# Batch 0's loads ahead of everything else, TensorE transposes for all of batch 1, and probabilities times values as one matmul per head in two column groups

## The chip, the cores and the metric

The kernel runs on one core of a Trainium2 chip. The metric is the time of one execution on the device, in microseconds; lower is better. The profile is one further execution, taken by the hardware profiler. Its engines are TensorE (PE for matmuls, PEld for the weight loads that run beside them), VectorE (DVE), ScalarE (ACT), GpSimd (POOL) and the queue that issues DMAs (SP). The core has 16 DMA engines. PEclk is the share of its full clock that TensorE was granted.

## What is computed

Attention with a window of 32 in two kinds of mask, and then a feed-forward block whose input is first mixed along the sequence by a product of rank 32:

```
q, k, v: (8 batches, 8 heads, 576, 64); U (576,32), V (32,576); w_ch1 (512,2048), w_ch2 (2048,512)
scores = q k^T / 8                     # heads 0-3: 0 <= i-j < 32
                                       # heads 4-7: 0 <= i-j < 128 and (i-j) % 4 == 0
attn = exp(scores - max); attn /= sum(attn) + 1e-9
x = attn v, heads side by side         # (8, 576, 512)
u = x + (x^T U V)^T
out = u + relu(u w_ch1) w_ch2
```

## The kernel before

Tokens of the dilated heads are permuted so that their mask becomes a window of 32 as well. A **group** is four units of work; a unit is 64 queries of two heads at once. A batch has NGB = 9 groups, numbered g through all eight batches, so that batch 0 is g = 0 to 8 and batch 1 is g = 9 to 17.

Each group passes through these steps:

- `score` (L368): one matmul per unit. For batches 0 and 1 it is an f32 matmul of 128 rows (L392): q of the two heads stands in 128 weight columns, 96 keys stream past. Later batches use another layout and fp32r (L381), but for one group per batch.
- `soften` (L395): VectorE adds the mask and takes the maximum (L412), ScalarE takes the exponential and its sum (L416).
- `turn` (L424): the probabilities are transposed into `pt`. For g below PE_T = 12 TensorE does it, four transposes per group (L429) and one copy by VectorE (L433). From there on VectorE does it, eight block transposes per group (L445, or L442 where the group is wide).
- `weighted` (L448): the product with v. For each unit one f32 matmul (L453) with `pt` of both heads as 128 weight columns and v of both heads as 128 streamed columns. It computes a 128x128 result, of which the two 64x64 blocks on the diagonal, one per head, are used. An f32 matmul appears in the trace as two records with a weight load each. VectorE then multiplies by the reciprocal of the sum (L481) and writes into x, or for the dilated heads into `xp`, which DMAs scatter into x (L485).

After its nine groups a batch is mixed with U and V: `split` (L493), the matmuls of `t_mm` (L508, line 521, 64 weight columns each), `mix` (L539).

The feed-forward block runs over 12 chunks of 384 tokens. In each chunk, 16 slices of the hidden layer follow each other: `layer1` (L742, matmul L748) and `layer2` (L758, matmul L765), which make up most of TensorE's work. Between their matmuls `slot()` hands out the pieces of the attention of later batches: `queue` gives each piece a place in units of chunks. Batch 1 lies within chunk 0 (places 0 to HI1 - MARGIN = 0.55), batch 2 begins after it, and so on at a rate of a batch in 1.5 chunks.

**The beginning.** Before chunk 0, batch 0's attention and mixing run by themselves, with the preparation of the weights beside them. `weight_step` (L267) loads a piece of U, V or the 64-bit weights (L200, L202) and narrows it on ScalarE, VectorE and GpSimd. Loads are issued by SP in order. FETCH = 5 groups of q and k and four of v are issued ahead; `pre` (L591) issues the others while the groups run, into QKS = 4 buffers for q and k and VBS = 7 for v, in a pool `early` that is closed when batch 0 is done. From NE = 7 on q and k come in pairs of units instead, through `fetch` (L333), into TB = 3 buffers of the tag `qks`. The constant `wide_sb`, masks for batch 2 and later, has a place of its own from the start. Tile's scheduler orders the instructions of each engine at build time, so they need not stand in program order.

Of the kernel before, what the change touches and what calls it, by code (L numbers as in the profile page):

```python
# [10 lines left out]
F32 = mybir.dt.float32  # L11
F32R = mybir.dt.float32r
BF16 = mybir.dt.bfloat16
# [7 lines left out]
B, H, S, D = 8, 8, 576, 64  # L21
# [5 lines left out]
P = 128  # L27
QB = 64
NJ = S // QB
KB = QB + WIN  # L30
# [10 lines left out]
UNITS = 4  # L41
QK1 = P + KB
KW = P + WIN
# [4 lines left out]
NGB = len(TILES) // 2  # L48
# [11 lines left out]
H_ON_ACT = 3  # L60
XL_DVE = ((0, 1), (1, 1))
AHEAD = 2
FETCH = 5
POST_AT = 0.7
TAIL = 0.25
BLK = P // WIN
ZS = 2
NE = 7
QKB = 3
AHEAD_AT = 0.9  # L70
LO0 = 0.1
TB = 3
# [14 lines left out]
F_LAST = 13  # L87
RAWS = 4
VS = 4
QKS = 4  # L90
XPS = 4
VBS = 7
DVE_FROM = 2
TURN_AT = 0.5
TURN_GAP = 0.08
PT_ACT = ()
PE_T = 12
MASK_AT = (None, -16, 0, 16, 32, 48)
WIDE_AT = (None, 0, 16, 32, 48)
NEG = -8.0e9  # L100
# [50 lines left out]
def attention_moe_kernel(ctx: ExitStack, tc: tile.TileContext, qk1, qk2, vv, masks, wide, ident, ut, vt, w1, w2, out):  # L151
    nc = tc.nc

    const = ctx.enter_context(tc.tile_pool(name="const", bufs=1))
# [9 lines left out]
    def make_w(lo, hi, side):  # L164
        pool = tc.tile_pool(name=f"w{lo}", bufs=1, side=side)
        pool = ctx.enter_context(pool)
        n = hi - lo
        t1 = [pool.tile([P, KC, n * P], F32R, name=f"w1{i}_{lo}") for i in "hl"]
        t2 = [pool.tile([P, n, DM], F32R, name=f"w2{i}_{lo}") for i in "hl"]
        for f in range(lo, hi):  # L170
            fs = slice((f - lo) * P, (f - lo + 1) * P)
            held_w[f] = [t[:, :, fs] for t in t1] + [t[:, f - lo, :] for t in t2]

    HM = len(MASK_AT) // 2
    mask_sb = [work.tile([P, HM, KB], F32, tag="qk", name=f"mask{i}", bufs=QKB) for i in range(2)]
    spare = work.tile([P, QK2], F32, tag="qk", name="spare", bufs=QKB)
    wide_sb = const.tile([P, len(WIDE_AT), KW], BF16, name="wide_sb")
    id_sb = const.tile([P, P], F32, name="id_sb")
    us = const.tile([P, 9, 2 * RANK], F32R, name="us")
    vs = const.tile([P, P + S], F32R, name="vs")  # L180
# [117 lines left out]
    loaded = {}  # L298

    def load_qk(g):  # L300
        if g >= NE:
            if g == NE:
                for i in range(0, 2 * TB, 2):
                    fetch(UNITS * g + i)
        elif (g, 0) not in loaded:
            t = early.tile([P, UNITS, QK1], F32, tag="qk", name=f"qk{g}", bufs=QKS)
            nc.sync.dma_start(out=t, in_=qk1[g])
            loaded[g, 0] = t

    def load_v(g, i):  # L310
        if (g, 1, i) not in loaded:
            us_ = slice(2 * i, 2 * i + 2)
            if g < NGB:
                if i == 0:
                    t = early.tile([KB, UNITS, P], F32, tag="v", name=f"v{g}", bufs=VBS)
                    nc.sync.dma_start(out=t, in_=vv[g])
                    loaded[g, 1, 0] = t[:, 0:2]
                    loaded[g, 1, 1] = t[:, 2:4]
            else:
                t = work.tile([KB, 2, P], F32, tag="v", name=f"v{g}_{i}", bufs=3)  # L320
                nc.sync.dma_start(out=t, in_=vv[g][:, us_])
                loaded[g, 1, i] = t
# [10 lines left out]
    def fetch(n):  # L333
        if n >= UNITS * NG or n in raws:
            return
        if n < N2:
            if n % 2 == 0:
                raw = work.tile([P, 2, QK1], F32, tag="qks", name=f"qkr{n}", bufs=TB)
                nc.sync.dma_start(out=raw, in_=qk1[n // UNITS][:, n % UNITS:n % UNITS + 2])
                raws[n] = raw[:, 0]  # L340
                raws[n + 1] = raw[:, 1]
        else:
            raw = work.tile([P, QK2], F32, tag="qk", name=f"qkr{n}", bufs=QKB)
            m = QK1 if is_odd(n) else QK2
            nc.sync.dma_start(out=raw[:, 0:m], in_=qk2[n - N2][:, 0:m])
            raws[n] = raw
# [100 lines left out]

    def weighted(g, pt, ssum):  # L448
        b = g // NGB
        pv = psum.tile([P, UNITS, P], F32, tag="ps", name=f"pv{g}")  # L450
        for u in range(UNITS):
            v_sb = loaded[g, 1, u // 2]
            nc.tensor.matmul(pv[:, u, :], lhsT=pt[:, u, :], rhs=v_sb[:, u % 2, :], start=True, stop=True)  # L453
        nc.vector.tensor_scalar(out=ssum, in0=ssum, scalar1=1e-9, scalar2=None, op0=ALU.add)
        nc.vector.reciprocal(out=ssum, in_=ssum)
        moves = []
        xp = None
        for i in range(2):
            half, j = tile_of(g, 2 * i)
            us_ = slice(2 * i, 2 * i + 2)  # L460
            cs = slice(half * HALF_D, (half + 1) * HALF_D)
            if half == 0:
                t, row = divmod(b * S + j * QB, P)
                dst = x_tile(t)[row:row + QB, cs]
            else:
                if xp is None:
                    if b == 0:
                        xp = early.tile([P, HALF_D], F32, tag="xp", name=f"xp{g}", bufs=XPS)
                    elif b < SPLIT and g % 2:
                        xp = spare[:, 0:HALF_D]  # L470
                    else:
                        xp = work.tile([P, HALF_D], F32, tag="xp", name=f"xp{g}", bufs=1)
                    part = next(p for p, js in enumerate(DPART) if j in js)
                row = QB * DPART[part].index(j)
                dst = xp[row:row + QB]
                moves += [(t, to, n, row + r) for r, t, to, n in runs_of(b, half, j)]
            dst4 = dst.rearrange("p (u h d) -> p u h d", u=2, h=2)
            for h in range(2):
                rs = slice(QB * h, QB * (h + 1))
                norm = ssum[QB * i:QB * (i + 1), h::2] if is_wide(g) else ssum[rs, us_]  # L480
                nc.vector.tensor_tensor(  # L481
                    out=dst4[:, :, h, :], in0=pv[rs, us_, h * D:(h + 1) * D],
                    in1=norm.unsqueeze(2).broadcast_to([QB, 2, D]), op=ALU.mult)
        for t, to, n, r in sorted(moves):
            nc.sync.dma_start(out=x_tile(t)[to:to + DIL * (n - 1) + 1:DIL, HALF_D:], in_=xp[r:r + n])  # L485
        if moves and b == 0:
            split(b, part, 1, xp, slice(0, QB * len(DPART[part])))
# [96 lines left out]
    def batch_items(b):  # L584
# [3 lines left out]
        for s in range(NGB + LAG):  # L588
            g = NGB * b + s

            def pre(s=s, g=g):  # L591
                if b == 0:
                    for i in (g, g + 1, g + FETCH):
                        if i < NGB:
                            load_qk(i)
                    if g + FETCH - 1 < NGB:
                        load_v(g + FETCH - 1, 0)
                if 0 < s <= NGB:
                    load_v(g - 1, 0)
                if s >= LAG:  # L600
                    weighted(g - LAG, *held.pop(g - LAG))
                if b > 0 and 0 < s <= NGB:
                    load_v(g - 1, 1)

            def post(s=s, g=g):
                late = g - (NGB * b < PE_T)
                if late in state and late not in turned:
                    turned.add(late)
                    p_sb, _, ssum, _ = state.pop(late)
                    held[late] = (turn(late, p_sb), ssum)  # L610

            def some(us, g=g):
                for u in us:
                    score(g, u)
                for u in us:
                    n = UNITS * g + u
                    if n >= N2:
                        split_qk(n + LOOK)
                        fetch(n + LOOK + DMA_LOOK)
                    elif n >= UNITS * NE and n % 2 and n + 2 * TB - 1 < N2:  # L620
                        fetch(n + 2 * TB - 1)
                for u in us:
                    soften(g, u)

            step = UNITS if b < SPLIT else STEP
            units = [lambda us=range(u, u + step), some=some: some(us) for u in range(0, UNITS if s < NGB else 0, step)]
            if b < SPLIT:
                attn.append([lambda pre=pre, units=units, post=post: (pre(), [x() for x in units], post())])
            else:
                attn.append([pre] + units + [post])  # L630
# [43 lines left out]
    early_open = ExitStack()  # L674
    early = early_open.enter_context(tc.tile_pool(name="early", bufs=1))
    held_u.append(early.tile([P, len(DPART), 2 * RANK], F32R, name="us_d"))
    for g in range(FETCH):
        load_qk(g)
        if g == 0:
            for i in range(2):  # L680
                nc.sync.dma_start(out=mask_sb[i], in_=masks[:, HM * i:HM * (i + 1)])
        if g == 1:
            nc.sync.dma_start(out=id_sb, in_=ident)
        if g < FETCH - 1:
            load_v(g, 0)
    pre = batch_items(0)
    w_prio = [tc.cur_priority + W_OFF]
    for i, (_, it) in enumerate(pre):
# [11 lines left out]
    for _ in range(PRE_N):  # L700
        weight_step(NSMALL, NPIECE)
    tc.cur_priority = now
    early_open.close()
    make_w(F_MID, F_LAST, None)

    def ahead(stage):
# [164 lines left out]
```

## Time and profile before

| | |
|---|---|
| time, median of 3 runs | 1032.8 us (1031.57 to 1034.27) |
| the profiled execution's own time | 1032.92 us |
| its span in the trace | 1031.1 us |
| mean granted TensorE clock | 0.974 |
| first matmul of chunk 0 | at 69.54 us |
| first matmul of chunk 1 | at 177.86 us |

The span is the time between the first and the last instruction that the profiler saw; the 1.8 us that the run's own time is longer lie around it. Busy time counts each instruction from its start to its end. Consecutive matmuls overlap, so their durations add up to more than the time they take: what one costs in a row of its kind is read from the distance between starts. Below, "a group costs" means that distance summed over its records.

### The profile page before, as it was taken

Reading aid. Unit: us, or ns where it says so; the run is one execution under the profiler, and the core shown is the slowest. Engines: PE = TensorE matmul, PEld = TensorE weight load, DVE = VectorE, ACT = ScalarE, POOL = GpSimd, SP = SyncE. Lnnn points to the kernel's source line nnn. Section 1 sums busy time; section 2 is a strip of 40 time slices with the busy share of each in tenths; the row PEclk is TensorE's granted clock in tenths of the full one; section 3 lists DMA queues with packets and bytes.
Section 4 is the critical chain, followed back from the end, with each engine's and each line's share of the span. In section 5 each row is a group of like instructions: output and inputs, shape, how many; then the busy total and the mean of one; then the engine's idle time right before and its main releaser. Section 6 shows DMA issues by size and latency. Waiting matters only on the chain.

```text
span 1031.1 us, 17355 instructions
## 1 busy us (share of the span) xinstructions
PE 992.3 (96%) x5304; PEld 894.4 (87%) x5304; DVE 643.8 (62%) x2197; ACT 436.8 (42%) x1274; POOL 323.4 (31%) x519
## 2 busy tenths in 40 slices
PE   6769998999999999999999999999999999999998
PEld 5658887998899899998899898999889898999996
DVE  5888987877457863877557864777647874311211
ACT  5888874454244432444233532544324442111110
POOL 1476644353132630434122621335213431000000
PEclk9658999999999999999999999999999999999999
DMA  9767544243232433333232432424223321400000
GB/s 281 215 197 231 173 142 118 78 128 87 78 98 71 123 84 78 108 104 99 72 96 80 128 82 61 131 82 126 85 73 86 119 65 30 125 1 1 31 1 31
DMA packets 97197, 103.05 MB, mean 100 GB/s; under 512 B 12848, under 2 KB 84080, under 8 KB 97104
## 3 DMA queue, kind: packets, MB, share of 16 engines
q1 hardware_dynamic: 97104, 101.94, 34.6%
q8 instruction: 43, 0.70, 0.3%
q14 instruction: 50, 0.41, 0.1%
HBM read 79.86 MB, written 17.30 MB: 94 GB/s over the span
## 4 chain that ended last, share of the span: by engine, by line
PE 82%; DVE 10%; DMA 4%; ACT 3%; issue 1%; SPq 0%; POOL 0%; DVEq 0%; POOLq 0%; ACTq 0%
PE ph L748 36%; PE acc L765 35%; PE pv L453 5%; PE s L381 3%; PE t L521 2%; DVE pt L445 2%; DMA qk<-qk 1%; PE s L392 1%; DVE utl L582 1%; DMA qkr<-qk 1%; DMA v<-vv 1%; DVE v L217 1%; PE m L545 1%; ACT p L416 1%; DVE xp L481 1%
## 5 line engine op out<-in xcount | busy, mean ns | idle before, releaser
L765 PE MATMUL acc<-w2h,hh 128*128 128x512 f32 x576 | 229.4, 398 | 0.0
L765 PE MATMUL acc<-w2l,hh 128*128 128x512 f32 x576 | 228.5, 397 | 0.0
L357 POOL TENSOR_TENSOR qks<-qkr,qks 128x160 fp32r<-128x160 f32 x192 | 104.5, 544 | 376.8 <-ACT qks L356 254.4
L765 PE MATMUL acc<-w2h,hl 128*128 128x512 f32 x576 | 213.4, 397 | 1.6 <-DVE hl L754 1.6
L753 ACT ACTIVATE hh<-ph 128x384 fp32r<-128x384 f32 x192 | 93.6, 487 | 284.4 <-PE ph L748 274.6
L754 DVE SCALAR_TENSOR_TENSOR hl<-ph,hh 128x384 fp32r<-128x384 f32 x192 | 106.0, 552 | 167.5 <-ACT hh L753 167.0
L416 ACT ACTIVATE p<-p,nmax 128x160 f32<-128x160 f32 (+1 forms) x288 | 117.2, 408 | 137.4 <-DVE nmax L412 135.3
L748 PE MATMUL ph<-uth,w1h 128*128 128x384 f32 x768 | 175.3, 342 | 0.0
L748 PE MATMUL ph<-uth,w1l 128*128 128x384 f32 x768 | 174.6, 340 | 0.0
L748 PE MATMUL ph<-utl,w1h 128*128 128x384 f32 x768 | 173.3, 339 | 0.0
L748 PEld LDWEIGHTS ph<-uth,w1h 128*128 128x128 f32 x768 | 139.5, 190 | 15.0 <-ACT uth L581 0.3
L748 PEld LDWEIGHTS ph<-uth,w1l 128*128 128x128 f32 x768 | 136.8, 189 | 0.5
L748 PEld LDWEIGHTS ph<-utl,w1h 128*128 128x128 f32 x768 | 135.8, 188 | 1.5
L765 PEld LDWEIGHTS acc<-w2h,hl 128*128 128x128 f32 x576 | 108.1, 189 | 24.4 <-DVE hl L754 2.5
L442 DVE STREAM_TRANSPOSE pt<-p 32x128 f32<-32x128 f32 x384 | 115.9, 302 | 19.7 <-ACT p L416 14.5
L765 PEld LDWEIGHTS acc<-w2h,hh 128*128 128x128 f32 x576 | 109.2, 190 | 15.6 <-ACT hh L753 0.2
L765 PEld LDWEIGHTS acc<-w2l,hh 128*128 128x128 f32 x576 | 109.1, 189 | 14.8
L356 ACT CAST qks<-qkr 128x288 fp32r<-128x288 f32 x192 | 81.7, 430 | 84.7 <-PE s L381 58.7
L360 POOL TENSOR_TENSOR qks<-qkr,qks 64x128 fp32r<-64x128 f32 x192 | 90.1, 470 | 15.1
L409 DVE TENSOR_TENSOR p<-s,wide_sb 128x160 f32<-128x160 f32 x192 | 60.6, 319 | 46.6 <-PE s L381 44.6
L453 PE MATMUL pv<-v,pt 96*128 96x128 f32 x576 | 80.1, 283 | 3.8 <-DVE pt L445 1.7
L453 PEld LDWEIGHTS pv<-v,pt 96*128 96x128 f32 x576 | 77.2, 199 | 7.1 <-DVE pt L433 2.0
(68 smaller groups left out, 1052.9 us busy)
## 6 DMA issues: line engine op xcount, KB each, us to landing
qkr<-qk SPq DMA_DIRECT2D x192, 144.0 KB, 2.2
raw<-w SPq DMA_DIRECT2D x26, 512.0 KB, 5.1
v<-vv SPq DMA_DIRECT2D x126, 96.0 KB, 2.1
out<-x SPq DMA_DIRECT2D x36, 256.0 KB, 2.3
zd<-z SPq DMA_DIRECT2D x120, 64.0 KB, 1.9
xt<-zd SPq DMA_DIRECT2D x30, 256.0 KB, 2.8
qkr<-qk SPq DMA_DIRECT2D x22, 224.0 KB, 3.4
qk<-qk SPq DMA_DIRECT2D x7, 448.0 KB, 7.7
```

The lines of the kernel that those rows point to most:

```text
L356: nc.scalar.copy(out=t[:, 0:QK2], in_=raw)
L357: nc.gpsimd.tensor_tensor(out=t[:, QK2:], in0=raw[:, P:], in1=t[:, P:QK2].bitcast(F32), op=ALU.subtract)
L360: eng.tensor_tensor(out=t[lo, 0:P], in0=raw[lo, 0:P], in1=t[lo, 0:P].bitcast(F32), op=ALU.subtract)
L381: nc.tensor.matmul(sp, lhsT=t[:, 0:P], rhs=t[:, P:], start=True, stop=True)
L409: nc.vector.tensor_tensor(out=p_sb[:, u, :], in0=sp[:, 0:KW], in1=wide_sb[:, kind], op=ALU.add)
L416: nc.scalar.activation(out=p_sb[:, u, 0:w], in_=p_sb[:, u, 0:w], func=AF.Exp, bias=nmax[:, u:u + 1], scale=-1.0, accum_out=ssum[:, u:u + 1],)
L442: nc.vector.transpose(out=to[:, :, WIN * (r % 2):WIN * (r % 2 + 1)], in_=p_sb[rs, :, QB * s + WIN * k:QB * s + WIN * (k + 1)])
L453: nc.tensor.matmul(pv[:, u, :], lhsT=pt[:, u, :], rhs=v_sb[:, u % 2, :], start=True, stop=True)
L748: nc.tensor.matmul(ph, lhsT=w[:, k, :], rhs=u[:, k, :], start=(n == 0), stop=(n == len(seq) - 1))
L753: nc.scalar.activation(out=hh, in_=ph, func=AF.Relu)
L754: nc.vector.scalar_tensor_tensor(out=hl, in0=ph, scalar=0.0, in1=hh.bitcast(F32), op0=ALU.max, op1=ALU.subtract)
L765: nc.tensor.matmul(acc[i], lhsT=h[:, ss], rhs=w, start=(f == 0 and n == 0), stop=(f == FC - 1 and n == 2))
```

## The change

- Batch 0's nine groups of q, k and v are all issued first, in the order of the groups. q and k have nine buffers (QKS = 9, NE = 9), and v takes tiles of the pool `x` (16 buffers of 128 x 512 f32, of which the other users are the x tiles). The first half of the masks and the identity follow group 0's q and k, the second half follows group 2's. `pre` issues none of batch 0's loads any more. FETCH and VBS are gone. U, V, the weights and batch 1's first three pairs of q and k follow.
- PE_T is 18 instead of 12: groups 12 to 17, the last six of batch 1, are transposed by TensorE too, with VectorE's copy of line 433.
- `weighted` issues two matmuls for each unit, one per head: 64 weight columns of `pt`, 64 streamed columns of v. Head 0's result goes to partitions 0 to 63 and head 1's to partitions 64 to 127 of a tile of 4 x 64 columns, half as wide as before.
- `wide_sb` lives in a pool `rest` that is opened when `early` has been closed.

```diff
-FETCH = 5
-NE = 7
+NE = 9
-QKS = 4
+QKS = 9
-VBS = 7
-PE_T = 12
+PE_T = 18
...
     def load_qk(g):
-        if g >= NE:
-            if g == NE:
-                for i in range(0, 2 * TB, 2):
-                    fetch(UNITS * g + i)
-        elif (g, 0) not in loaded:
+        if (g, 0) not in loaded:
             t = early.tile([P, UNITS, QK1], F32, tag="qk", name=f"qk{g}", bufs=QKS)
...
-                    t = early.tile([KB, UNITS, P], F32, tag="v", name=f"v{g}", bufs=VBS)
+                    t = xpool.tile([P, UNITS, P], F32, tag="x", name=f"v{g}")[0:KB]
                     nc.sync.dma_start(out=t, in_=vv[g])
...
     def weighted(g, pt, ssum):
         b = g // NGB
-        pv = psum.tile([P, UNITS, P], F32, tag="ps", name=f"pv{g}")
+        pv = psum.tile([P, UNITS, D], F32, tag="ps", name=f"pv{g}")
         for u in range(UNITS):
             v_sb = loaded[g, 1, u // 2]
-            nc.tensor.matmul(pv[:, u, :], lhsT=pt[:, u, :], rhs=v_sb[:, u % 2, :], start=True, stop=True)
+            for h in range(2):
+                hs = slice(h * D, (h + 1) * D)
+                nc.tensor.matmul(pv[QB * h:QB * (h + 1), u, :], lhsT=pt[:, u, QB * h:QB * (h + 1)],
+                                 rhs=v_sb[:, u % 2, hs], start=True, stop=True)
...
-                    out=dst4[:, :, h, :], in0=pv[rs, us_, h * D:(h + 1) * D],
+                    out=dst4[:, :, h, :], in0=pv[rs, us_, :],
...
             def pre(s=s, g=g):
-                if b == 0:
-                    for i in (g, g + 1, g + FETCH):
-                        if i < NGB:
-                            load_qk(i)
-                    if g + FETCH - 1 < NGB:
-                        load_v(g + FETCH - 1, 0)
                 if 0 < s <= NGB:
                     load_v(g - 1, 0)
...
-    for g in range(FETCH):
+    for g in range(NGB):
         load_qk(g)
         if g == 0:
-            for i in range(2):
-                nc.sync.dma_start(out=mask_sb[i], in_=masks[:, HM * i:HM * (i + 1)])
-        if g == 1:
+            nc.sync.dma_start(out=mask_sb[0], in_=masks[:, 0:HM])
             nc.sync.dma_start(out=id_sb, in_=ident)
-        if g < FETCH - 1:
-            load_v(g, 0)
+        if g == 2:
+            nc.sync.dma_start(out=mask_sb[1], in_=masks[:, HM:])
+        load_v(g, 0)
...
     tc.cur_priority = now
+    for i in range(0, 2 * TB, 2):
+        fetch(UNITS * NGB + i)
     early_open.close()
+    rest = ctx.enter_context(tc.tile_pool(name="rest", bufs=1))
+    wide_sb = rest.tile([P, len(WIDE_AT), KW], BF16, name="wide_sb")
```

More of the change, by code (lines that the diff above doesn't have):

```diff
@@ L176, in attention_moe_kernel @@
     spare = work.tile([P, QK2], F32, tag="qk", name="spare", bufs=QKB)
-    wide_sb = const.tile([P, len(WIDE_AT), KW], BF16, name="wide_sb")
     id_sb = const.tile([P, P], F32, name="id_sb")
```

## The prediction

> **What bounds the kernel now.** I read the page first (span, slices), then the windows of the three stages, then waits and timeline inside each.
>
> ```profile
> span 1031.1 us, 17355 instructions
> PE   6769998999999999999999999999999999999998
> DVE  5888987877457863877557864777647874311211
> PEclk9658999999999999999999999999999999999999
> ```
>
> From the fourth slice on TensorE is busy 80% of a slice or more, and from the fifth on at nearly its full clock. VectorE is as busy in the first six slices (26 us each), and later mostly at 40 to 80%. So the run has a beginning in which no engine is full and a long rest that belongs to TensorE. The windows are cut at the first matmul of chunk 0 and of chunk 1 (columns: length, busy us and instructions of PE, PEld, DVE, ACT, POOL, then the granted clock, DMA share, GB/s):
>
> ```profile
> 0.00:69.50 69.50, 45.94 (x222) 38.34 (x223) 52.98 (x177) 49.31 (x142) 29.12 (x30) 0.73 0.78 235
> 69.50:177.80 108.30, 99.81 (x541) 88.17 (x540) 87.69 (x267) 82.43 (x221) 63.80 (x59) 0.94 0.55 167
> 177.80:1031.10 853.30, 846.55 (x4543) 767.86 (x4542) 503.17 (x1754) 305.11 (x914) 230.44 (x432) 1.00 0.29 80
> ```
>
> The first stage is batch 0 and the first weights: no engine is bound, the clock is 0.73. The second is chunk 0 with batch 1 in it. The third, 853 us, is TensorE's: 847 us busy, VectorE at 59%. In that third stage the largest wait that the list of waits has for a matmul is this one, so what is taken off TensorE's queue there comes off the end:
>
> ```profile
> PE acc L765 <- DVE hl L754: 1.6, 3, 0.6
> ```
>
> **Probabilities times values (pv), the term that decides.** One group in the third stage, with its neighbours (columns: start, time, count at the end):
>
> ```profile
> 303.68 0.31 PE L381 MATMUL s<-qks 128*128 128x320 f32 x1
> 303.83 1.05 PE L453 MATMUL pv<-v,pt 96*128 96x128 f32 x8
> 304.64 0.60 PE L748 MATMUL ph<-uth,w1h 128*128 128x384 f32 x2
> L453 PE MATMUL pv<-v,pt 96*128 96x128 f32 x576 | 80.1, 283 | 3.8 <-DVE pt L445 1.7 <-DVE pt L433 1.4 <-issue 0.6
> ```
>
> Eight records last 1.05 us from first start to last end, one alone 0.28 us (the mean of the last row). So starts lie (1.05 - 0.28) / 7 = 0.110 us apart, and a group costs 8 x 0.110 = 0.88 us.
>
> After the change a group has 16 records of 64 streamed columns. What one of them streams for comes from another f32 matmul, with 96 columns:
>
> ```profile
> 324.99 0.36 PE L392 MATMUL s<-qkr 128*128 128x96 f32 x2
> L392 PE MATMUL s<-qkr 128*128 128x96 f32 x136 | 22.1, 287 | 2.3 <-DMA qkr<-qk 2.3
> ```
>
> 0.36 - 0.28 = 0.080 us between its starts (the mean of 0.287 holds batch 0's at a lower clock, so one is taken as long as a pv record), so 128 columns take 0.110 and 96 take 0.080: in proportion, 64 take 0.055. One after another, 16 x 0.055 = 0.88 us: the change then saves nothing, since two heads of 64 columns stream as long as one matmul of 128. All of the gain must come from the two heads' halves of the array working at the same time. If they do, the order hi, lo of head 0, hi, lo of head 1 lets each second record start beside the first of the other head: 9 slots instead of 16, 9 x 0.055 = 0.50 us. The weight loads set another floor: the L392 records each load 128 columns and still start 0.080 us apart, so a load of 64 takes at most about 0.040 us, and 16 in a row at most 0.64 us. I take 0.57, between the two, as nothing in the trace shows two halves loading at once: 0.31 us saved per group, with 0.38 and 0.24 as the ends of this case.
>
> Whether halves cost something when TensorE enters and leaves them can be read from the mixing matmuls, which use 64 weight columns already (128*64 is rows by columns of the array):
>
> ```profile
> 236.13 0.69 PE L748 MATMUL ph<-uth,w1l 128*128 128x384 f32 x3
> 236.66 0.86 PE L521 MATMUL t<-xhl,us 128*64 128x256 f32 x6
> 237.36 0.34 PE L748 MATMUL ph<-uth,w1l 128*128 128x384 f32 x1
> ```
>
> Three ph take 236.66 - 236.13 = 0.53 us to the start of t, 0.177 each. The six t take 0.70 us to the start of the next ph, 0.117 each. Neither border shows anything extra, and weight loads of 64 columns stay hidden. What the trace doesn't show is an output on partitions 64 to 127 and the alternation between halves. Cost in the third stage, batches 2 to 7, 54 groups: 54 x 0.31 = 16.7 us less, all on TensorE's path, which had hardly a wait. The next engine in line there is VectorE, at 59%.
>
> **Batch 1's transposes.** Removed from VectorE are 6 groups x 8 block transposes, added are 6 copies there and 24 transposes on TensorE:
>
> ```profile
> L445 DVE STREAM_TRANSPOSE pt<-p 32x128 f32<-32x128 f32 x96 | 28.9, 301 | 3.9 <-ACT p L416 2.7
> L433 DVE COPY pt<-ptp 96x512 f32<-96x512 f32 x12 | 8.2, 682 | 3.0 <-PE ptp L429 2.7
> 15.96 0.27 PE L429 MATMUL ptp<-id_sb,p 128*96 128x128 f32 x1
> 17.56 0.38 PE L429 MATMUL ptp<-id_sb,p 128*96 128x128 f32 x2
> ```
>
> VectorE: 48 x 0.301 = 14.4 us away, 6 x 0.682 = 4.1 added, 10.3 us less of its 87.7 in chunk 0. TensorE: two in 0.38 us, less one alone (0.27), are 0.11 apart, so 24 x 0.11 = 2.6 us more. Behind each transpose on TensorE's queue stands the feed-forward; it waits if ScalarE's exponentials are late. But `turn` runs one group late, so they had a whole group's time. What VectorE's slowness costs TensorE now:
>
> ```profile
> 118.92 1.16 PE L453 MATMUL pv<-v,pt 96*128 96x128 f32 x8 [1.71 <-DVE pt L445]
> 120.79 0.78 PE L765 MATMUL acc<-w2h,hh 128*128 128x512 f32 x1
> 123.50 0.63 PE L765 MATMUL acc<-w2h,hh 128*128 128x512 f32 x1
> 241.03 0.40 PE L765 MATMUL acc<-w2l,hh 128*128 128x512 f32 x1
> 241.26 0.39 PE L765 MATMUL acc<-w2h,hl 128*128 128x512 f32 x1
> ```
>
> TensorE idles 1.71 us until 118.92. Soon after, seven acc matmuls stand between the starts 120.79 and 123.50, both counted, 2.71 / 6 = 0.45 us apart, where the third stage has 0.23 (the last two rows): half a clock, 6 x 0.22 = 1.3 us. I let both go with the wait: 3.0 us. With batch 1's own pv (9 x 0.31 = 2.8 us, by the sum above) and the 2.6 us added, chunk 0 becomes 3.2 us shorter. The ends of that: all 10.3 us of VectorE's time plus the 2.8, or, if the wait only moves to ScalarE, 0.2 us.
>
> The Trainium skill, TensorE: Matmul & The Clock Gate, Part 1, says that the clock is halved after an idle window of about 3.4 us. The idle time in the row is half as long, so by that rule the slow stretch had another cause and would stay: the time would then be 1.3 us longer.
>
> **Batch 0's loads.** Batch 0's later groups were fetched late:
>
> ```profile
> 2.60 0.42 SPq L307 DMA_DIRECT2D qk<-qk  x1
> 9.99 0.35 SPq L202 DMA_DIRECT2D raw<-ut  x1
> 18.22 0.33 SPq L307 DMA_DIRECT2D qk<-qk  x1
> 39.32 0.35 SPq L339 DMA_DIRECT2D qkr<-qk  x1
> 36.86 0.69 PE L392 MATMUL s<-qkr 128*128 128x96 f32 x4
> DVE p L412 <- PE s L392: 10.7, 5, 6.3
> qk<-qk SPq DMA_DIRECT2D x7, 448.0 KB, 7.7
> v<-vv SPq DMA_DIRECT2D x9, 192.0 KB, 7.7
> 19.06 0.62 ACT L209 ACTIVATE v<-raw 128x448 f32<-128x448 f32 x1 [0.75 <-DMA raw<-ut]
> 10.00:20.00 10.00, 9.90 (x67) 9.40 (x65) 7.01 (x44) 4.50 (x20) 0.00 (x0) 1.00 1.04 309
> ```
>
> The seventh group's q and k are issued at 18.22 us and the ninth group scores at 36.86. All nine now need 9 x (448 + 192) KB, about 5.9 MB: at the 309 GB/s of the last row, 19 us and, from the first issue on, some 21 us. Then VectorE is the next bound of batch 0. Its idle time in the first stage is 69.5 - 53.0 = 16.5 us; of that the first 6 pass before any score can exist, so about 10 can go at most. Of the 10.7 us in which it waits for scores, the first 6.3 is that same beginning, so some 4.4 us are the loads'. I take 4 us off the first matmul of chunk 0, ends 0 and 9. Each load moved forward is a load that U, V and the weights now stand behind: SP takes about 0.42 us apiece, 21 with masks and identity in some 9 us, so U's load is issued near 10 us as before (9.99), but lands behind 5.9 MB at some 22 us, where ScalarE now has it at 19.06: 3 us later. Covered by VectorE's and ScalarE's attention work of those microseconds; without that cover 3 us come back. Batch 1's first pairs and `wide_sb` go behind them too; they are first needed in chunk 0 and after it.
>
> The remaining edits are free: the pv tile half as wide is read in the same pieces (64 x 128 elements each), and v's tiles are given back to pool `x` before the weights' last pieces or batch 1's x need all 16.
>
> **The sum**, against the profiled execution's own 1032.9 us, which is 0.1 us from the median of the three runs: 1032.9 - 16.7 - 3.2 - 4 = 1009.0 us. With all ends good: 54 x 0.38 = 20.5, 13.1 and 9 less, 990; all bad but halves still parallel: 54 x 0.24 = 13, 0 and +3, 1023.
>
> **The rivals.**
>
> *The halves don't overlap.* Then a group stays at 0.88 us, or 0.96 if a record takes 0.060. For: no row of this trace shows two matmuls streaming at once. Against: nothing in the trace either; that the two heads use different weight columns and different partitions only makes it possible. Time: 0 to +5 us over 63 groups, chunk 0 without its 2.8 (0.4 left) and the loads as forecast: 1032.9 - 0.4 - 4 = 1028.5, to 1033.
>
> *Entering and leaving the halves drains TensorE.* There is one change of shape in the trace that does cost, to half of the rows:
>
> ```profile
> 241.78 0.30 PE L381 MATMUL s<-qks 128*128 128x320 f32 x1
> 242.02 0.33 PE L521 MATMUL t<-xhl,us 64*64 64x256 f32 x1
> 242.28 0.62 PE L748 MATMUL ph<-uth,w1h 128*128 128x384 f32 x2
> ```
>
> The s streams 0.15 us (303.68 to 303.83 above) and t starts 0.24 later, 0.09 more; t would take 0.117 and ph starts 0.26 later, 0.14 more. A round trip of 0.23 us, in 63 groups 14.5 us, turns 1009 into 1023. Against it: the 128*64 rows above show none of that. The Trainium skill, TensorEngine Tiling (Array Packing), Key Properties, says that changing the tiling mode, not just the tile, drains TensorE, and also that different tiles work in parallel. By the first the result would be this rival's; the 64*64 rows agree with it, the 128*64 rows don't.
>
> *Slower: the weight load of the other half can't be hidden.* If a load into the other half has to wait for the stream before it, each of the 16 records costs its stream and its load, with the nearest row 0.080 us: 16 x 0.080 = 1.28 us a group, 0.40 more than now. Over 63 groups 25 us: 1032.9 + 25 - 0.4 - 4 = 1053.5. It decides from the point at which the 4.4 us gained elsewhere are used up, 4.4 / 63 = 0.07 us a group, 0.060 us a record. For: 16 loads instead of 8, and f32's two records. Against: 64-column loads were hidden among the six t.
>
> **How the numbers follow.** About 0.3%, 3 us, is what a measurement of this kernel can tell from no change. Parallel halves without a drain: 0.60, since the loads and borders in the trace allow it and only parallelism itself isn't shown. No overlap: 0.20. Drain with overlap: 0.08. Slower: 0.12. Faster is the first and third case and most of the second's better half (0.08): 0.75. Within 0.3% the rest of the second: 0.12. Slower 0.13. The range runs from 1000, half the way from 1009 to all good ends (990), to 1031, which holds most of the no-overlap case (1028.5 to 1033); left out are the slower case and those outer ends.
>
> **What would show it.** pv: a group's 16 records within about 0.57 us and their neighbours undisturbed; chunks 1 to 9 shorter by about 6 x 0.31 = 1.9 us each. Transposes: no block transposes before chunk 1, VectorE some 10 us less there, no wait of pv for `pt`. Loads: the ninth group's score near 25 to 30 us instead of 36.86, first matmul of chunk 0 near 65.5. Wrong it is if pv's starts lie 0.055 us or more apart in sum, if gaps surround pv, or if chunk 0 begins no earlier because the weights or VectorE are late.

## The result and the profile after

| | before | after |
|---|---|---|
| median | 1033.26 us (6 runs, 1031.57 to 1034.27) | 1024.41 us (6 runs, 1021.52 to 1025.8) |
| ratio, 95% interval | | 0.9916 (0.9900 to 0.9933) |
| the profiled execution's own time | 1032.92 us | 1025.73 us |
| first matmul of chunk 0 | 69.54 us | 63.39 us |
| chunk 0, to the first matmul of chunk 1 | 108.3 us | 109.0 us |
| from there to the end of the span | 853.2 us | 851.6 us |

The change is faster by 8.9 us, 0.8%. The forecast was 24 us. The page of the changed kernel, in the lines shown of the one before:

```profile
span 1024.0 us, 18519 instructions
PE   6569998999999999999999999999999999999998
DVE  4977777887458854876557963777547874311211
PEclk9679998999999999999999999999999999999999
```

The picture is the same: TensorE holds the run from the fourth slice on, and nothing in these digits says what the halves did. The windows say where the time went, cut at the first matmuls of chunks 0 and 1 of this kernel:

```profile
0.00:63.39 63.39, 37.41 (x292) 28.32 (x292) 45.48 (x169) 39.27 (x125) 19.92 (x24) 0.78 0.74 218
63.39:172.39 109.00, 100.51 (x639) 86.13 (x639) 82.00 (x234) 91.10 (x238) 73.06 (x66) 0.94 0.61 192
172.39:1024.00 851.61, 844.38 (x4975) 747.29 (x4974) 504.39 (x1754) 303.33 (x913) 229.36 (x430) 1.00 0.28 80
```

Of the span's 7.1 us, 6.1 come from the beginning (forecast: 4), chunk 0 gives back 0.7 (forecast: 3.2 gained), and the third stage, where 16.7 were expected, yields 1.6. These 1.6 are less than the product itself gave there, for the third stage of the changed kernel begins at half the clock, and that of the kernel before did not. The first 4.2 us of the stage, the changed kernel's first:

```profile
172.39:176.60 4.21, 4.21 (x14) 4.21 (x14) 3.96 (x16) 1.70 (x7) 1.96 (x4) 0.50 0.46 127
177.86:182.10 4.24, 4.24 (x24) 4.24 (x25) 4.13 (x17) 1.87 (x7) 2.53 (x6) 1.00 0.62 168
```

Half of 4.2 us is 2.1; without that the stage would be some 3.7 us shorter.

One group of the product, with its neighbours in the queue:

```profile
206.34 0.34 PE L741 MATMUL ph<-uth,w1h 128*128 128x384 f32 x1
206.61 0.69 PE L448 MATMUL pv<-v,pt 96*64 96x64 f32 x16
207.22 0.61 PE L741 MATMUL ph<-uth,w1h 128*128 128x384 f32 x2
207.68 0.31 PE L374 MATMUL s<-qks 128*128 128x320 f32 x1
L448 PE MATMUL pv<-v,pt 96*64 96x64 f32 x1152 | 51.3, 232 | 2.9 <-DVE pt L426 2.7 <-DMA v<-vv 0.2
```

The 16 records last 0.69 us, one alone 0.23: their starts are 0.46 / 15 = 0.031 us apart on average, where one after another would need 0.055. (Single starts, which the row merges, come in twos 0.007 us apart; from one pair to the next it is 0.058 us, and 0.107 from the first to the second pair.) So the two halves do work at the same time. At that pace the 16 need 0.46 + 0.06 = 0.52 us. The loss is at the borders. A ph streams 0.175 us, but the product starts 206.61 - 206.34 = 0.27 us after it: 0.09 late. From its start to the next ph pass 0.61 us, 0.09 more than the 0.52, and the two ph that follow take 207.68 - 207.22 = 0.46 us instead of 0.35: 0.11 late. The visit costs 0.09 + 0.61 + 0.11 = 0.81 us, of which 0.29 are borders, against 0.88 before. (Counted in this way the group of the kernel before, at 303.83 us, costs the same 0.88 or 0.89: it starts 0.15 us after the s, which is not late, the ph follows after 0.81, and the two ph last 0.60 us, where two in a row last 0.177 + 0.34 = 0.52: 0.08 late.)

### The profile page after: what moved, and what is told of

The parts are those of the page before. It is cut to its first block, busy times and chain, and to the rows that moved or that the text cites. A ratio compares the mean times of both kernels' runs of the same rounds, so it can differ in the third digit from the quotient of the medians.

```text
span 1024.0 us, 18519 instructions
## 1 busy us (share of the span) xinstructions
PE 982.3 (96%) x5904; PEld 861.7 (84%) x5904; DVE 631.9 (62%) x2155; ACT 433.7 (42%) x1274; POOL 322.3 (31%) x519
## 4 chain that ended last, share of the span: by engine, by line
PE 85%; DVE 6%; DMA 5%; ACT 3%; issue 1%; SPq 0%; DVEq 0%
PE ph L741 38%; PE acc L758 36%; PE pv L448 3%; PE s L374 3%; PE t L517 2%; DMA qk<-qk 2%; DMA qkr<-qk 2%; PE m L541 1%; PE s L385 1%; DMA raw<-w 1%; DVE xhl L497 1%; DVE utl L578 1%; DVE pt L438 1%; ACT v L206 1%; ACT sign L208 1%
## 5 line engine op out<-in xcount | busy, mean ns | idle before, releaser
L758 PEld LDWEIGHTS acc<-w2h,hl 128*128 128x128 f32 x576 | 107.4, 189 | 24.8 <-DVE hl L747 2.8
L435 DVE STREAM_TRANSPOSE pt<-p 32x128 f32<-32x128 f32 x384 | 115.8, 302 | 16.5 <-ACT p L409 11.2
L758 PEld LDWEIGHTS acc<-w2l,hh 128*128 128x128 f32 x576 | 108.7, 189 | 15.7
L497 POOL TENSOR_TENSOR xhl<-x,xhl 128x256 fp32r<-128x256 f32 (+1 forms) x70 | 52.9, 778 | 78.0 <-ACT xhl L495 61.5
L215 POOL TENSOR_TENSOR v<-v,sign 128x512 int32<-128x512 int32 (+2 forms) x35 | 45.5, 1300 | 57.6 <-ACT sign L208 39.2
```

Of the source, the lines that this page charges most:

```text
L215: nc.gpsimd.tensor_tensor(out=vi, in0=vi, in1=s32, op=ALU.add)
L435: nc.vector.transpose(out=to[:, :, WIN * (r % 2):WIN * (r % 2 + 1)], in_=p_sb[rs, :, QB * s + WIN * k:QB * s + WIN * (k + 1)])
L497: eng.tensor_tensor(out=xl[rs], in0=x[rs], in1=xh[rs].bitcast(F32), op=ALU.subtract)
L758: nc.tensor.matmul(acc[i], lhsT=h[:, ss], rhs=w, start=(f == 0 and n == 0), stop=(f == FC - 1 and n == 2))
```

## The experiments

The theory after the comparison: the halves stream side by side, as forecast, and each visit to the half-wide shape costs TensorE about 0.3 us in drains, which eats the gain. The rivals: the halves save in full and another part of the change gives it back; or the lost time at the borders has nothing to do with the shape.

Each kernel is compared with the kernel before on the same chip (medians; ratio with its 95% interval):

| kernel | time | before beside it | ratio |
|---|---|---|---|
| pv_alone | 1027.9 | 1032.1 | 0.9952 (0.9933 to 0.9970) |
| no_pv | 1025.6 | 1032.1 | 0.9940 (0.9920 to 0.9960) |
| pe12 | 1025.8 | 1032.1 | 0.9939 (0.9920 to 0.9958) |
| pe18_alone | 1031.3 | 1032.1 | 0.9983 (0.9966 to 1.0001) |
| loads_alone | 1026.7 | 1032.9 | 0.9943 (0.9925 to 0.9962) |
| one_half | 1050.0 | 1032.4 | 1.0169 (1.0140 to 1.0197) |
| head_outer | 1040.8 | 1032.4 | 1.0080 (1.0055 to 1.0105) |
| wide_mid | 1048.4 | 1032.4 | 1.0149 (1.0116 to 1.0181) |
| wide_end | 1038.1 | 1032.4 | 1.0048 (1.0026 to 1.0070) |
| t_f32 | 1074.6 | 1032.9 | one run |
| u_early | 1022.4 | 1032.9 | 0.9901 (0.9881 to 0.9921) |
| paired68 | 1019.1 | 1032.9 | 0.9872 (0.9847 to 0.9897) |
| act_less | 1023.5 | 1032.9 | 0.9919 (0.9903 to 0.9935) |
| best | 1018.6 | 1032.9 | 0.9865 (0.9849 to 0.9882) |

**The parts by themselves.** First the product alone:

```diff
 (kernel before)
+            for h in range(2): ... one matmul per head, as in the change
```

> The kernel before with only the product split into two column groups; loads and transposes as before. Theory (the two halves do stream side by side, which saves some 0.36 us a group, but each entry into the half-wide shape and each way out of it drains TensorE, some 0.32 us a group): 63 groups x 0.04 us, so 2 to 3 us faster than before, about 1030 to 1031 us. Rival (the halves save their 0.3 us a group in full and the loads or the transposes of the change give it back): 17 us faster, about 1016.

Measured 1027.9, 4.2 us faster: a little more than the theory's 2 to 3, far from the rival's 17. Then the change without it:

```diff
 (changed kernel)
-            for h in range(2): ...
+            nc.tensor.matmul(pv[:, u, :], lhsT=pt[:, u, :], rhs=v_sb[:, u % 2, :], start=True, stop=True)
```

> The changed kernel with the product as one matmul of 128 columns per unit again; new loads and all of batch 1's transposes on TensorE stay. Theory (drains eat the saving of the halves): 2 to 3 us slower than the changed kernel, about 1027 us, the first matmul of chunk 0 still near 63 us. Rival (the halves save in full): 17 us slower, about 1041, slower than the kernel before.

Measured 1025.6; by the ratios, 0.9940 against 0.9916, 2.5 us slower than the changed kernel, and the intervals overlap. The rival's 1016 and 1041 are out: the product is worth some 2 to 5 us, not 17, and no other part of the change gives anything of that size back. The profiled executions agree: the third stage lasts 853.2 to 855.4 us in the four kernels with one matmul per unit (before, no_pv, pe18_alone, loads_alone) and 850.5 to 851.7 in the five with the product as in the change (changed, pv_alone, pe12, u_early, act_less).

```diff
 (changed kernel)
-PE_T = 18
+PE_T = 12
```

> The changed kernel with VectorE transposing groups 12 to 17 again. Theory (in chunk 0 ScalarE's narrowing of weights became the last to be done, so VectorE's 10 us are off the path and TensorE pays 2.6 us for the transposes): between 2 us faster and 1 us slower than the changed kernel, 1022 to 1025. Rival (the transposes give back what VectorE's wait cost, as forecast): 3 us slower or more, 1027 or above.

```diff
 (kernel before)
-PE_T = 12
+PE_T = 18
```

> The kernel before with only groups 12 to 17 transposed by TensorE. Theory of the forecast for this part by itself: 3.0 us of a wait and its half clock go, 2.6 us are added, so within 1 us of before, 1032 to 1034, VectorE some 10 us less busy in chunk 0. Rival (chunk 0 waits for VectorE more widely): up to 10 us faster, 1023. Other rival (the transposes wait for ScalarE on TensorE's queue): 2.6 us slower or more, 1036.

By the ratios the transposes are worth 2.4 us in the change (pe12, 0.9939 against 0.9916) and 1.8 us alone, and neither can be told from nothing; pe12 lies between its two expectations and tells no more. VectorE is relieved about as worked out: in chunk 0 of pe18_alone, from 66.57 to 173.16 us, it is busy 79.23 us, 8.5 fewer than the 87.69 of the kernel before.

```profile
66.57:173.16 106.59, 99.41 (x565) 89.15 (x565) 79.23 (x226) 82.07 (x223) 63.70 (x60) 0.95 0.56 171
```

The loads without the two other parts:

```diff
 (changed kernel)
-PE_T = 18
+PE_T = 12
-            for h in range(2): ...
+            nc.tensor.matmul(pv[:, u, :], lhsT=pt[:, u, :], rhs=v_sb[:, u % 2, :], start=True, stop=True)
```

> The kernel before with only the new order and buffers of the loads (and wide_sb's later place); product and transposes as before. Theory (the loads carry most of the change's gain): chunk 0 begins 6 us earlier, of which 1 us is lost in chunk 0, where ScalarE now has the weight pieces that it used to narrow before it: 5 us faster than before, 1027 to 1028. Rival (their gain is all lost in chunk 0, as the work is only moved): 1032 to 1033.

Measured 1026.7, 6.2 us faster: the loads carry most of the change. Alone, the three parts take off 0.48%, 0.17% and 0.57%, together 1.2%; the change with all three takes off 0.84%. Some of it may overlap, but the intervals are nearly as wide as the difference.

**The borders.** Is it the shape? One small matmul over all 128 columns goes into each group, once in the middle and once at the end (its result isn't used):

```diff
 (changed kernel)
-        pv = psum.tile([P, UNITS, D], F32, tag="ps", name=f"pv{g}")
+        pv = psum.tile([P, UNITS + 1, D], F32, tag="ps", name=f"pv{g}")
...
+            if u == 1:          # wide_mid; wide_end: u == 3
+                nc.tensor.matmul(pv[:, UNITS, 0:32], lhsT=id_sb, rhs=id_sb[:, 0:32], start=True, stop=True)
```

> The changed kernel with one small matmul over all 128 columns (32 columns streamed, its result unused) between units 1 and 2 of each group, so that each group leaves and enters the half-wide shape twice. Theory (each leaving and entering costs some 0.3 us): 0.3 us and 0.06 us for the matmul itself in 63 groups, some 23 us slower than the changed kernel, 1047. Rival (the gaps at the borders are not caused by the shape): as the next one, 1028.

> Control of the one before: the same small matmul after unit 3, where the shape changes anyway. Theory: only its own 0.06 us in 63 groups, 4 us slower than the changed kernel, 1028. Rival (the small matmul itself costs): as the one before.

A group of wide_mid, then one of wide_end:

```profile
199.80 0.31 PE L374 MATMUL s<-qks 128*128 128x320 f32 x1
200.04 0.45 PE L448 MATMUL pv<-v,pt 96*64 96x64 f32 x8
200.42 0.41 PE L451 MATMUL pv<-id_sb 128*128 128x32 f32 x2
200.76 0.45 PE L448 MATMUL pv<-v,pt 96*64 96x64 f32 x8
201.14 0.61 PE L743 MATMUL ph<-uth,w1l 128*128 128x384 f32 x2
```

```profile
195.35 0.31 PE L374 MATMUL s<-qks 128*128 128x320 f32 x1
195.59 0.69 PE L448 MATMUL pv<-v,pt 96*64 96x64 f32 x16
196.21 0.41 PE L451 MATMUL pv<-id_sb 128*128 128x32 f32 x2
196.45 0.60 PE L743 MATMUL ph<-uth,w1l 128*128 128x384 f32 x2
```

In wide_mid 1.10 us pass from the first product record to the ph, in wide_end 0.86. The same work, one visit more: 0.24 us. The small matmul itself costs more than I expected (0.86 instead of 0.61 us), so wide_end is 10 us slower than expected. The difference of the two times, 10.3 us over 63 groups or 0.16 each, is smaller than the 0.24 of the rows; the intervals of the two ratios allow both. The third stages of the two profiled executions, 875.2 and 861.1 us, are 14.1 apart, 0.26 in each of the 54 groups. One more visit does cost, so the gaps belong to the shape.

Is it the second half?

```diff
 (changed kernel)
-        pv = psum.tile([P, UNITS, D], F32, tag="ps", name=f"pv{g}")
+        pv = psum.tile([P, 2, UNITS, D], F32, tag="ps", name=f"pv{g}")
...
-                nc.tensor.matmul(pv[QB * h:QB * (h + 1), u, :], ...
+                nc.tensor.matmul(pv[0:QB, h, u, :], ...
...
-                    out=dst4[:, :, h, :], in0=pv[rs, us_, :],
+                    out=dst4[:, :, h, :], in0=pv[0:QB, h, us_, :],
```

> The changed kernel with both heads' results on partitions 0 to 63, so that all 16 records use the same half of the columns, as the mixing matmuls do. Theory (what drains TensorE is the use of the second half; work in the first half alone enters and leaves for nothing, as in the mixing matmuls): no pairs, 16 x 0.056 = 0.90 us a group and no gap at either border, 0.09 us more than the changed kernel's 0.81 over 63 groups: some 6 us slower than it, 1030. Rival (any f32 work with 64 weight columns drains): 0.90 + 0.32 us a group, 26 us slower, 1050.

```profile
196.17 0.31 PE L374 MATMUL s<-qks 128*128 128x320 f32 x1
196.41 1.15 PE L448 MATMUL pv<-v,pt 96*64 96x64 f32 x16
197.49 0.62 PE L741 MATMUL ph<-uth,w1l 128*128 128x384 f32 x2
197.94 0.36 PE L385 MATMUL s<-qkr 128*128 128x96 f32 x2
```

My theory of the second half fell: the time is the rival's, 1050.0. The s streams 0.15 us, the product starts 0.24 after it; the two ph take 0.45 instead of 0.35. The borders are those of the changed kernel although only the first half is used, as in the mixing matmuls that had shown none. And 16 records in one half take (1.15 - 0.23) / 15 = 0.061 us each from start to start, with the first one late, instead of 0.031: it is the other half that pairs them.

What then sets the mixing matmuls apart? They are fp32r, with 128 rows.

```diff
 (changed kernel)
-                t_ps[b, c], lhsT=u[rs], rhs=m[rs],
+                t_ps[b, c], lhsT=u[rs].bitcast(F32), rhs=m[rs].bitcast(F32),
```

> The changed kernel with the mixing matmuls of U in f32 instead of fp32r, same shapes: two records of 256 columns each instead of one. Only their borders matter. Theory (it is f32 that makes work with 64 weight columns drain TensorE, also in the first half and with 128 rows): the matmul before the first of a run is followed by its successor some 0.09 us late, and the matmul after the last one likewise, where fp32r showed nothing. Rival (the drain belongs to the 96 rows of the probabilities): no gap here. In time each of some 106 such matmuls outside batch 0 takes 0.43 us instead of 0.117, 33 us, and 20 us more with a drain at each of some 60 borders: 1058 without and up to 1078 with drains.

```profile
263.69 0.39 PE L758 MATMUL acc<-w2h,hh 128*128 128x512 f32 x1
263.92 0.40 PE L758 MATMUL acc<-w2l,hh 128*128 128x512 f32 x1
264.25 0.65 PE L517 MATMUL t<-xhl,us 128*64 128x256 f32 x2
264.82 0.44 PE L741 MATMUL ph<-utl,w1h 128*128 128x384 f32 x1
```

The acc before the t starts 0.23 us before its successor acc, but the t comes 0.33 us after that one: 0.10 late, in the same shape 128*64 that had no gap in fp32r. The two t records take 0.57 us to the ph, where 2 x 0.216 would do (256 columns at the f32 pace of the product, 0.055 us for 64, give 0.22): 0.14 late. The ph itself lasts 0.44 us, where one behind another ph lasts 0.34. So it is f32 in 64 weight columns, not the rows or the half; f32 alone doesn't do it, as the 128-column product of the kernel before enters without a gap. The time, 1074.6 us in a single execution, lies near the theory's upper number, 1078.

**Do pairs need neighbours?**

```diff
 (changed kernel)
-        for u in range(UNITS):
-            for h in range(2):
+        for h in range(2):
+            for u in range(UNITS):
```

> The changed kernel with the loops of the product exchanged: all units of head 0, then all of head 1, so that neighbours in the queue share a half. Theory (the pairs come from neighbours in different halves; matmuls start in order): starts 0.056 us apart except at the change of head, borders as in the changed kernel, 0.4 us more a group, some 25 us slower than the changed kernel, 1050. Rival (the halves work apart however they are queued): as the changed kernel, 1024.

```profile
199.25 0.31 PE L374 MATMUL s<-qks 128*128 128x320 f32 x1
199.49 0.97 PE L448 MATMUL pv<-v,pt 96*64 96x64 f32 x16
200.39 0.62 PE L741 MATMUL ph<-uth,w1l 128*128 128x384 f32 x2
```

From the first product record to the ph pass 0.90 us: more than the 0.61 of the changed kernel, less than one_half's 1.08. So 1040.8 lies between the two expectations. Single starts show why: twelve of the fifteen distances are 0.052 us or more and three are 0.004 to 0.006. The first of these three stands between the fifth and the sixth start. The sixth record lasts 0.270 us, as otherwise only the first of a half does (the first one in one_half, the first two in the changed kernel), where all others last 0.222: it is the first of head 1, and it starts ahead of the last three of head 0, which the kernel issues before it. So the halves need not be neighbours in the queue, and these matmuls do not start strictly in order, as the theory had it; but five of head 0's eight had started alone.

**Using it.** If a visit costs by itself, two groups in one visit should cost one drain:

```diff
 (changed kernel; from batch 2 on)
+            def both(s=s, g=g):        # at place i + 0.68 of every other step
...
+                gs = [i for i in (g - LAG, g - LAG + 1) if i < NGB * (b + 1)]
+                pvs = [product(i, held[i][0]) for i in gs]
+                for i, pv in zip(gs, pvs):
+                    weighted(i, *held.pop(i), pv=pv)
...
-                t = work.tile([KB, 2, P], F32, tag="v", name=f"v{g}_{i}", bufs=3)
+                t = work.tile([KB, 2, P], F32, tag="v", name=f"v{g}_{i}", bufs=6)
...
-                        xp = work.tile([P, HALF_D], F32, tag="xp", name=f"xp{g}", bufs=1)
+                        xp = work.tile([P, HALF_D], F32, tag="xp", name=f"xp{g}", bufs=2)
```

The maxima and sums of the softmax also get a third buffer from batch 1 on.

> The changed kernel with the products of two groups issued together from batch 2 on (five visits to the half-wide shape per batch instead of nine; v is loaded one step earlier into six buffers, xp has two). Theory (each visit costs 0.35 us beside 16 or 32 records in pairs 0.058 us apart): a double visit takes 1.28 us instead of 2 x 0.82, 24 of them save 8.6 us, and the later work of VectorE gives perhaps 2 back: 1016 to 1018. Rival (the gaps belong to each group, say to its wait for the transposes, not to the visit): as the changed kernel, 1024, or slower by VectorE's bunched work.

```profile
186.87 0.39 PE L776 MATMUL acc<-w2h,hl 128*128 128x512 f32 x1
187.10 0.39 PE L776 MATMUL acc<-w2h,hh 128*128 128x512 f32 x1
187.42 1.15 PE L447 MATMUL pv<-v,pt 96*64 96x64 f32 x32
188.50 0.50 PE L776 MATMUL acc<-w2l,hh 128*128 128x512 f32 x1
188.84 0.39 PE L776 MATMUL acc<-w2h,hl 128*128 128x512 f32 x1
```

A double visit costs 0.32 - 0.23 = 0.09, then 188.50 - 187.42 = 1.08, then 0.34 - 0.23 = 0.11: 1.28 us, instead of 2 x 0.81. The kernel takes 1019.1 us, 5.3 us less than the changed kernel (4.5 by the ratios), some 60% of the 24 x 0.34 = 8.2 us that the visits save. The theory of a price per visit holds; its 1016 to 1018 was a little low. Where the rest went is in the third stage and in the waits of its matmuls:

```profile
171.58:1017.40 845.82, 834.65 (x4975) 744.14 (x4974) 503.08 (x1754) 299.81 (x913) 227.93 (x430) 1.00 0.29 81
PE acc L776 <- DVE ssum L456: 2.6, 2, 1.4
PE ph L759 <- DVE utl L583: 2.2, 3, 0.8
```

The stage is 5.8 us shorter than the changed kernel's, although TensorE is idle for 845.8 - 834.7 = 11.2 us of it instead of 7.2, in waits for VectorE above all. No kernel has the added buffers without the pairing; but where TensorE was idle for 7.2 us and is now for 11.2, it isn't the buffers that took its time off.

**The beginning and chunk 0.**

```diff
 (changed kernel)
-PRE_AT = range(1, 7)
+PRE_AT = range(1, 6)
         load_v(g, 0)
+        if g == 4:
+            weight_step(0, NSMALL)
```

> The changed kernel with the loads of U and of the first half of V issued after the fifth group's q, k and v instead of after all nine. Theory (SP could not issue U's load until 19 us since the queue was full, and ScalarE stood idle half of the time from 20 to 30 us): ScalarE narrows U and V some 5 us earlier and has a piece of weight or two less to do in chunk 0: 2 to 4 us faster than the changed kernel, 1021 to 1022. Rival (what binds the beginning is VectorE and the attention itself): the four last groups come 2 us later, and nothing is gained or 2 us are lost, 1024 to 1026.

```profile
8.01 0.33 SPq L199 DMA_DIRECT2D raw<-ut  x1
9.26 0.33 SPq L199 DMA_DIRECT2D raw<-vt  x1
20.00:30.00 10.00, 8.74 (x90) 7.59 (x89) 9.46 (x49) 7.43 (x32) 1.15 (x2) 0.83 1.05 290
```

U's load is issued at 8.01 us and ScalarE (the fourth of the counts) is busy 7.43 us between 20 and 30. In the changed kernel it is 4.84. SP's issues there come 0.5 to 1.7 us apart from 8.82 us on, 1.1 on average, and U's load stands behind them:

```profile
8.82 0.33 SPq L309 DMA_DIRECT2D v<-vv  x1
9.75 0.33 SPq L300 DMA_DIRECT2D qk<-qk  x1
11.19 0.33 SPq L309 DMA_DIRECT2D v<-vv  x1
...
17.40 0.33 SPq L309 DMA_DIRECT2D v<-vv  x1
19.08 0.33 SPq L199 DMA_DIRECT2D raw<-ut  x1
20.00:30.00 10.00, 7.14 (x87) 5.62 (x85) 7.67 (x39) 4.84 (x20) 0.00 (x0) 1.00 1.04 311
```

The time, 1022.4, is 2 us below the changed kernel's, near the theory's range, but the two intervals overlap. By the start of chunk 0, at 59.39 us instead of 63.39, ScalarE has prepared 10 pieces of the weights, as many as in the changed kernel: they come earlier, but chunk 0 doesn't have fewer left. The last two kernels ask what binds chunk 0, and whether the gains add up:

```diff
 (changed kernel: act_less)
-H_ON_ACT = 3
+H_ON_ACT = 2
```

> The changed kernel with H_ON_ACT = 2 instead of 3: in one weight piece of four the cast moves from ScalarE (0.61 us) to VectorE (1.2 us). Theory (chunk 0 did not shorten since ScalarE's weight pieces bind it there: four more of them lie in it than before): some 8 casts, 5 us off ScalarE, 2 to 4 us faster than the changed kernel, 1020 to 1022. Rival (VectorE or TensorE's order binds chunk 0): VectorE's 10 us more make it 0 to 6 us slower, 1024 to 1030.

> The changed kernel with both the product of two groups in one visit and U's load issued after the fifth group. Theory (the two act in different stages and add up: 5 us in the third stage, 2 us before chunk 0): 1016 to 1018. Rival (what comes earlier in the beginning is lost again in chunk 0, so that only the pairing counts): 1019.

The kernel best has the edits of u_early and paired68 together. act_less took 1023.5, which is neither faster nor slower than the changed kernel by more than the runs scatter. It takes from ScalarE (87.7 us busy in chunk 0 instead of 91.1) what it gives to VectorE (90.8 instead of 82.0), so it shows that this exchange gains nothing, not that ScalarE's backlog is harmless. best, 1018.6, is not told apart from paired68; it is 1.35% (1.18 to 1.51) faster than the kernel before, and the earlier U adds nothing measurable to it.

## Why the prediction was wrong

**The step that failed** is "Neither border shows anything extra". The row was read rightly: fp32r work of 64 weight columns enters and leaves for nothing. It was carried over to f32 work of the same width, which it doesn't speak for. t_f32 shows that: the same matmuls in f32 have the gaps. With them a visit costs 0.81 us where I had taken 0.57, and the 54 groups of the third stage save 54 x (0.88 - 0.81) = 3.8 us instead of 16.7; the third stage of the profiled execution became 1.6 us shorter, or 3.7 without its beginning at half the clock. The prediction's own sign of being wrong, gaps around pv, is what came. Everything else in this term was right: the proportion by columns (0.055 forecast, 0.058 measured from pair to pair), the records two by two (eight pairs, where the forecast had nine steps), the hidden loads. Without the outer borders, 16 records would have cost the 0.52 us above, the good end of my case but for 0.02.

**The rival that came true** is the one I gave a chance of 0.08, the drain with overlap, at 1023 us. That its number lies 1.4 us from the measured 1024.4 is luck. By stages it had 4.3, 1.1 and 4 us off the third stage, chunk 0 and the beginning; measured are 1.6, -0.7 and 6.1. Its price of 0.23 us came from the row halves in fp32r, 64*64, and left out a part: the two ph behind that t last 0.62 us together, where two in a row last 0.177 + 0.34 = 0.52, so the round trip is 0.33, and at that price this rival would have stood near 1030. The visits show as much: 0.29 at the borders (0.09 before the product, 0.09 between its last records and the ph, 0.11 in the ph) and 0.05 more from the first pair to the second (0.107 against 0.058; in one_half and t_f32, too, the first spacing is the longest). The Trainium skill, TensorEngine Tiling (Array Packing), Key Properties, says both things that were found: tiles work in parallel, and a change of mode drains. I set the second against one row that differed and let the row decide; for f32 the rule was right, for fp32r in 64 columns the runs don't bear it out.

**Loads**: 4 us forecast, 6.1 at the first matmul of chunk 0, 6.2 in the time of loads_alone. The 6.1 are not sharp: pe18_alone, whose edit touches batch 1 alone, came to chunk 0 at 66.57 us where the kernel before took 69.54. The ninth group scores at 26.69 us instead of 36.86 (forecast: 25 to 30). But U's load is not issued near 10 us: SP gets to it at 19.08, as its issues come 1.1 us apart on average from about the ninth microsecond on (the rows of u_early's comparison). ScalarE pays for that: it has prepared 10 pieces before chunk 0 instead of 14:

```profile
L206 ACT ACTIVATE v<-raw 128x512 f32<-128x512 f32 (+2 forms) x10 | 6.3, 631 | 3.2 <-DMA raw<-ut 3.2
```

```profile
L209 ACT ACTIVATE v<-raw 128x512 f32<-128x512 f32 (+2 forms) x14 | 9.0, 645 | 3.5 <-DMA raw<-w 2.2 <-DMA raw<-ut 0.8 <-DMA raw<-vt 0.5
```

The first line is the changed kernel's, up to 63.39 us, the second that of the kernel before, up to 69.54. So a part of the earlier start is work moved into chunk 0, where ScalarE is busy 91.10 us instead of 82. What that costs isn't shown: in loads_alone, which moves the same work, chunk 0 lasted 107.4 us, no longer than before.

**Chunk 0**: 3.2 us shorter forecast, 0.7 longer measured. The wait of 1.71 us for VectorE's transposes is gone, but TensorE has new ones there:

```profile
PE tp L572 <- DVE nmax L405: 2.6, 2, 1.9
PE ptp L422 <- ACT p L409: 2.2, 1, 2.2
PE s L374 <- DVE x L543: 1.5, 1, 1.5
```

The second is the case that I had argued away: a transpose on TensorE's queue behind ScalarE's exponentials. So the step "I let both go with the wait" failed as well: by the windows TensorE is idle for 108.30 - 99.81 = 8.5 us of chunk 0 before and for 109.00 - 100.51 = 8.5 after, and the granted clock is 0.94 in both. The wait and the stretch at half the clock are gone from their places, but others came: at 169.70 us, behind the waits of tp, the clock falls to 0.5 until 176.6. Of the 3.0 us nothing was gained. Batch 1's product saved 9 x 0.07 = 0.6 instead of 2.8 us.

The transposes are not what lengthened chunk 0. In the profiled executions, one for each kernel, it lasts 106.6 us in pe18_alone against 108.3 before, 106.6 in no_pv against 107.4 in loads_alone, and 109.0 in the changed kernel against 111.2 in pe12: 0.8 to 2.2 us less with TensorE's transposes each time. With the new product it is the longer one each time: 108.7 in pv_alone against 108.3, 109.0 against 106.6, 111.2 against 107.4. Why, and what sets the length of chunk 0, stays open: relieving VectorE alone (pe18_alone) left the time within what the runs scatter, act_less relieved ScalarE only at VectorE's cost, and a kernel that relieves both at once wasn't tried.

Two smaller readings of the prediction were loose, and nothing rests on them: VectorE's first slice is half busy, not 80%, and the stretch at half the clock lasted from 120.7 to 124.1 us, which is worth 1.7 us, not 1.3.

## What to carry to other kernels

Splitting a matmul into column halves pays only for what runs side by side, less what each entry and exit costs: count the visits, and put as much half-wide work as can wait into one of them. A row of the trace vouches for its own type as much as for its shape, so take the price of an unseen operation from one in the same type, or hold both ends. And when loads are put ahead, look at when the ones behind them can be issued at all, and which engine then does its work later.

## What the runs showed of the hardware

- Two f32 matmuls of 64 weight columns in different halves run together: 16 records with starts 0.031 us apart on average, 0.061 in one half.
- Going from 128 to 64 weight columns and back cost about 0.3 us a visit in f32, in both halves or in the first alone, with 96 rows or 128, and nothing visible in fp32r with 128 rows.
- Matmuls of the two halves overlap even when three records lie between them in the queue, and then start out of its order (head_outer: 0.90 us for 16, against 0.61 alternating and 1.08 in one half).
- A full-width f32 matmul of 32 columns between half-wide work and the next ph put that ph 0.25 us later (0.86 against 0.61).
